# Signs of the last seven weight pieces, made on ScalarE and multiplied in by GpSimd

## The chip, the cores and the metric

The kernel runs on one core of a Trainium2 chip. The metric is the device time of one execution in microseconds (us). Engines are named as in the profile: PE (TensorE), with PEld for its weight loads, DVE (VectorE), ACT (ScalarE), POOL (GpSimd) and SP (SyncE, which issues transfers).

## What is computed

Three stages follow each other. The first is a gated linear attention over 768 positions of 4 batches with 8 heads of width 40; the second sends each of 3072 tokens to one of eight experts with a capacity of 384; the third is a dense layer with ELU between two weight matrices.

```python
for t in range(S):
    m_new = np.maximum(f_gate[:, :, t] + m, i_gate[:, :, t])
    f_stab = np.exp(f_gate[:, :, t] + m - m_new)
    i_stab = np.exp(i_gate[:, :, t] - m_new)
    C = f_stab[..., None, None] * C + i_stab[..., None, None] * np.einsum('bhd,bhe->bhde', vt, kt)
    n = f_stab[:, :, None] * n + i_stab[:, :, None] * kt
    y[:, :, t] = sigmoid(o_gate[:, :, t]) * einsum(C, qt) / np.maximum(np.abs(nq), 1.0)
...
out[mask] = np.maximum(x[mask] @ w1[e], 0.0) @ w2[e]
...
h = x @ w_in
g = np.where(h > 0.0, h, np.exp(np.minimum(h, 0.0)) - 1.0)
return g @ w_out
```

The two dense matrices `w_in` and `w_out` arrive as 64-bit floats. The kernel needs each as a sum of two 32-bit parts (high and low), so it has to turn 64-bit words into 32-bit ones first.

## The kernel before

**Attention** runs 24 steps (`Attention.run`, u = 0 to 23), each on 64 positions of two batches. In program order, which is also each engine's order, a step u issues: PE the recall of the next step and the scores of the one after it (L415, L311), a zeroing matmul (L385); DVE the weighting P (L380) and the seed of the output (L391) for the next step; PE the logits (L484), then the values and the state update (L401, L428); DVE the gates (L448 to L453) and the state sum C (L439); POOL the scaled output x (L454); PE a transpose of the former x (L470) and the decay (L322, L327), which ACT turns into xT (L472) and W (L329); POOL kt (L368), C (L370), and in every second step the mask product sel (L341). In every fourth step ACT also makes `keep` (L488) for a transpose of PE that comes ahead of the decay.

**Weights beside attention.** `Mlp.win_pieces` is a generator that makes 15 pieces of the dense weights while attention runs. Pieces 0 to 9 are of `w_in` (512 columns), 10 to 14 are of `w_out` (448 columns). `Attention.run` pulls it by `fill()` four times in each step from u = 2 on: once ahead of the gates and three times behind kt and C. Each `yield` ends what one such pull issues, so a pull decides in which place of every engine's order an instruction stands. One piece goes through `conv` (ACT: the absolute value into g, L1010, and a byte of the low word into F, L1017; DVE: the first xor with the sign bits, L1023, and in the next pull the second xor with g, L1026). In the pull after that ACT copies F as the high part (L1086, L1092 and L1094, or L1082), and then the low part is subtracted: by POOL for pieces 0 to 7 (L1088), by DVE for pieces 8 and 9 (L1096, L1098) and 10 to 14 (L1084). `conv` has a second way (`sign=True`), which `wout_pieces` already uses for nine later pieces of 320 columns: ACT also makes the Sign of the high word (L1012), and POOL multiplies it in (L1029).

Steps and pieces meet as follows in the trace: the xors of piece 8 stand behind the gates of step 12 (gates start at 91.86 us); of piece 9 on both sides of step 14's (102.92); piece 10 around those of 16 (114.73), piece 11 around those of 17 (118.78), piece 12 behind 18 (123.79), piece 13 behind 19 (130.14), piece 14 behind 20 (135.15) and ahead of 21's (139.71).

The buffers: `cx` (the 64-bit words) has three, `cg` and `cF` two each. The planner's estimates (`on`) in `conv` shape no order within attention.

Of the kernel before, what the change touches and what calls it, by code (L numbers as in the profile page):

```python
# [36 lines left out]
class Plan:  # L37
# [20 lines left out]
    def on(self, e, ns, after=0):  # L58

        self.at[e] = max(self.at[e], self.t, after) + ns  # L60
        return self.at[e] + HOP
# [899 lines left out]
class Mlp:  # L961
# [38 lines left out]
    def conv(self, wide, tiles, sign=False, top=False):  # L1000


        nc = self.nc
        x, g, F = tiles
        if not wide:
            return
        n = x.shape[1]
        hi = x[:, :, 1]
        on = self.plan.on
        nc.scalar.activation(g, hi.bitcast(F32), AF.Abs, scale=2.0**-112)  # L1010
        if sign:
            nc.scalar.activation(hi.bitcast(F32), hi.bitcast(F32), AF.Sign)  # L1012
        t = on("a", 967 if sign else 474)
        Fi = F.bitcast(I32)
        if top:
            b = x.rearrange("p n t -> p (n t)").bitcast(mybir.dt.uint8).rearrange("p (n t) -> p n t", t=8)
            nc.scalar.activation(Fi, b[:, :, 3], AF.Copy, scale=1 / 32, bias=-31 / 64)  # L1017
        else:
            nc.vector.tensor_scalar(Fi, x[:, :, 0], 29, None, op0=ALU.logical_shift_right)
            on("d", 310)  # L1020
        yield t, "d"
        if not sign:
            nc.vector.scalar_tensor_tensor(Fi, hi, -2**31, Fi, op0=ALU.bitwise_and, op1=ALU.bitwise_xor)  # L1023
            on("d", 484)
            yield self.plan.t, "d"
        nc.vector.scalar_tensor_tensor(Fi, g.bitcast(I32), 3, Fi, op0=ALU.logical_shift_left, op1=ALU.bitwise_xor)  # L1026
        t = on("d", 484)
        if sign:
            nc.gpsimd.tensor_tensor(F, F, hi.bitcast(F32), op=ALU.mult)  # L1029
            t = on("p", 890, t)  # L1030
        yield t, "ad"
# [7 lines left out]
    def win_pieces(self, stage):  # L1039

        nc = self.nc
        A, G = nc.scalar, nc.gpsimd
        wide = self.win.dtype != F32
        n = 512
        al, lo, up = slice(0, 128), slice(0, 64), slice(64, 128)
        tiles = {}
        total = 10 + EARLY * 320 // 448
        self.piece = self.got = 0

        def whole():  # L1050
            return stage.tile([128, n], F32, name="cF")

        def get(i):
            cs = slice(i * n, i * n + n)
            tiles[i] = [stage.tile([128, n, 2], I32, name="cx", bufs=3) if wide else None, None, None if wide else whole()]
            if i >= 10:
                cs = slice((i - 10) * 448, (i - 10) * 448 + 448)
                tiles[i] = [t if t is None else t[:, :448] for t in tiles[i]]
                loads = [(al, self.src(self.wout, al, cs))]
            else:  # L1060
                loads = [(al, self.src(self.win, al, cs))]
            self.fetch(loads, wide, tiles[i])

        def pull():
            if self.got < min(total, self.piece + 2 + wide):
                get(self.got)
                self.got += 1

        self.pull = pull
        for i in range(total):  # L1070
            self.piece = i
            while i not in tiles:
                yield
            k, h = divmod(i, 4)
            cs = slice((i - 10) * 448, (i - 10) * 448 + 448) if i >= 10 else slice(h * n, h * n + n)
            if wide:
                w = 448 if i >= 10 else n
                tiles[i][1:] = stage.tile([128, n], F32, name="cg")[:, :w], whole()[:, :w]
            F = tiles[i][2]
            yield from self.conv(wide, tiles.pop(i), top=True)  # L1080
            if i >= 10:
                A.activation(self.first[0][:, cs], F, AF.Copy)  # L1082
                yield
                nc.vector.tensor_tensor(self.first[1][:, cs], F, self.first[0][:, cs], op=ALU.subtract)  # L1084
            elif k < 2:
                A.activation(self.wih[:, k, cs], F, AF.Copy)  # L1086
                yield
                G.tensor_tensor(self.wil[:, k, cs], F, self.wih[:, k, cs], op=ALU.subtract)  # L1088
            else:
                w = self.wis.rearrange("p (k e t) -> p k e t", e=2, t=128)[:, 4 * h:4 * h + 4]  # L1090
                F = F.rearrange("p (k t) -> p k t", t=128)
                A.activation(w[lo, :, 0], F[lo], AF.Copy)  # L1092
                yield
                A.activation(w[up, :, 1], F[up], AF.Copy)  # L1094
                yield
                nc.vector.tensor_tensor(w[up, :, 0], F[lo], w[lo, :, 0], op=ALU.subtract)  # L1096
                yield
                nc.vector.tensor_tensor(w[lo, :, 1], F[up], w[up, :, 1], op=ALU.subtract)  # L1098
            yield
# [641 lines left out]
```

## Time and profile before

| What | Value |
|---|---|
| three runs | 745.18, 745.80, 748.81 us, median 745.80 |
| profiled execution | 748.99 us, of it 747.2 us span |
| attention | to about 152 us of the span |
| busy in the span | PE 697.8, DVE 558.0, ACT 395.5, POOL 198.9 us |
| busy from 0 to 152 us | PE 127.35, DVE 125.27, ACT 76.50, POOL 87.43 us |
| granted clock, mean | 0.970 |

The averages over the span hide the stages: behind attention PE is busy almost without a pause, and inside it several engines take turns. Each row of a timeline tells the start, the reported duration, the engine, the line, and what is written from what; in brackets stands how long the engine was idle ahead of it and which instruction ended that. Reported durations of neighbours can overlap by some hundredths.

### The profile page before, as it was taken

The numbers are of one execution on the slowest core, as the hardware profiler recorded it, in microseconds if no ns is written. First come the engines' busy times: TensorE is split into PE (matmuls) and PEld (weight loads), VectorE is DVE, ScalarE is ACT, GpSimd is POOL, SyncE is SP. The second block draws the span as 40 slices with busy tenths as digits, with TensorE's granted clock in tenths as the row PEclk, the third lists the DMA queues.
The fourth block names the chain that finished last, engine by engine and source line by source line (L and its number), as shares of the span: only waits on it lengthen the run. The fifth ranks groups of instructions, "written<-read, shape, count | busy, mean of one in ns | idle before, by whom it ended". The sixth has DMA issues, their size and how long they took to land.

```text
span 747.2 us, 17816 instructions
## 1 busy us (share of the span) xinstructions
PE 697.8 (93%) x7106; PEld 638.2 (85%) x7118; DVE 558.0 (75%) x1656; ACT 395.5 (53%) x894; POOL 198.9 (27%) x251
## 2 busy tenths in 40 slices
PE   7779889846999999999999999999999999999997
PEld 4656566635989998999899999999999999999997
DVE  8686999876888978986897688778867863752542
ACT  5544555434454727662675367456736763752443
POOL 5665766336211400410121022104100441001001
PEclk9998999955999999999999999999999999999999
DMA  8776878236101400410230023003200532100000
GB/s 280 237 211 195 262 237 257 65 115 195 41 1 52 157 1 1 139 62 10 73 109 28 1 86 97 28 1 114 72 25 1 172 106 76 37 1 27 1 1 26
DMA packets 21634, 67.28 MB, mean 90 GB/s; under 512 B 3504, under 2 KB 6576, under 8 KB 21552
## 3 DMA queue, kind: packets, MB, share of 16 engines
q1 hardware_dynamic: 13440, 35.12, 15.3%
q0 software_dynamic: 8064, 30.94, 12.6%
q8 instruction: 55, 0.90, 0.5%
q14 instruction: 27, 0.22, 0.1%
q10 hardware_dynamic: 48, 0.10, 0.0%
HBM read 58.28 MB, written 7.86 MB: 89 GB/s over the span
## 4 chain that ended last, share of the span: by engine, by line
PE 64%; issue 9%; DVE 7%; ACT 2%; DMA 2%; POOL 2%; POOLq 0%; SPq 0%; ACTq 0%; DVEq 0%
PE ph L1270 30%; PE acc L1423 6%; PE acc L1415 6%; PE acc L1416 6%; PE acc L1371 2%; PE acc L1365 2%; PE acc L1366 2%; PE acc L1363 1%; PE acc L1372 1%; DMA xd<-x 1%; PE ph L1223 1%; PE pr L843 1%; DMA stg<-in_w1b_dram,wi 1%; DVE e L1323 1%; POOL out_dram L1452 1%
## 5 line engine op out<-in xcount | busy, mean ns | idle before, releaser
L1323 DVE SCALAR_TENSOR_TENSOR e<-e,ph 128x384 f32<-128x384 f32 x128 | 70.1, 549 | 46.1 <-ACT e L1320 45.6
L1319 ACT ACTIVATE e<-ph 128x384 f32<-128x384 f32 x128 | 62.4, 487 | 76.5 <-PE ph L1270 66.6
L1270 PE MATMUL ph<-yh,wih 128*128 128x384 f32 x256 | 87.7, 343 | 0.0
L1270 PE MATMUL ph<-yh,wil 128*128 128x384 f32 x256 | 86.3, 337 | 0.0
L1147 DVE TENSOR_TENSOR gl<-e,gh 128x384 fp32r<-128x384 f32 x128 | 69.9, 550 | 2.3 <-ACT gh L1140 1.0
L1287 ACT ACTIVATE gh<-ph 128x384 fp32r<-128x384 f32 x62 | 30.5, 492 | 74.3 <-PE ph L1270 74.1
L1320 ACT ACTIVATE e<-e 128x384 f32<-128x384 f32 x128 | 67.3, 526 | 4.0
L1452 POOL DMA_INDIRECT out_dram<-ot,idx x24 | 24.7, 1031 | 160.3 <-ACT ot L1140 157.3
L1151 POOL DMA_INDIRECT stg<-in_w1a_dram,wi x16 | 16.0, 997 | 191.4 <-DVE wi L897 188.6
L1270 PE MATMUL ph<-yl,wih 128*128 128x384 f32 x256 | 65.2, 341 | 0.0
L1294 DVE SCALAR_TENSOR_TENSOR gl<-ph,gh 128x384 fp32r<-128x384 f32 x64 | 35.0, 552 | 38.5 <-ACT gh L1287 38.2
L1415 PE MATMUL acc<-woh,gh 128*128 128x320 f32 x186 | 56.2, 313 | 0.0
L1140 ACT ACTIVATE gh<-e 128x384 fp32r<-128x384 f32 x95 | 48.8, 514 | 13.4 <-DVE e L1323 13.2
L1416 PE MATMUL acc<-wol,gh 128*128 128x320 f32 x186 | 55.5, 309 | 0.0
L1415 PE MATMUL acc<-woa,gh 128*128 128x320 f32 x168 | 51.8, 318 | 0.5 <-DVE gh L1142 0.5
L1416 PE MATMUL acc<-wob,gh 128*128 128x320 f32 x168 | 50.4, 309 | 0.0
L1270 PEld LDWEIGHTS ph<-yh,wih 128*128 128x128 f32 x256 | 48.1, 188 | 0.2
L1270 PEld LDWEIGHTS ph<-yh,wil 128*128 128x128 f32 x256 | 48.2, 188 | 0.0
L1270 PEld LDWEIGHTS ph<-yl,wih 128*128 128x128 f32 x256 | 45.5, 188 | 0.0
L1270 PE MATMUL ph<-xh,w1h 128*128 128x384 f32 x128 | 43.6, 341 | 0.9 <-ACT xh L1140 0.7
L1270 PE MATMUL ph<-yh,wis 128*128 128x384 f32 x128 | 44.0, 344 | 0.0
L1270 PE MATMUL ph<-yl,wis 128*128 128x384 f32 x128 | 43.2, 337 | 0.0
(318 smaller groups left out, 2057.8 us busy)
## 6 DMA issues: line engine op xcount, KB each, us to landing
vk<-in_vk_dram SPq DMA_DIRECT2D x24, 484.0 KB, 5.0
qk<-in_qk_dram SPq DMA_DIRECT2D x20, 320.0 KB, 4.2
cx<-in_win_dram SPq DMA_DIRECT2D x10, 512.0 KB, 5.0
xd<-x SPq DMA_DIRECT2D x48, 80.0 KB, 3.5
wx<-in_wout_dram SPq DMA_DIRECT2D x9, 320.0 KB, 2.9
cx<-in_wout_dram SPq DMA_DIRECT2D x5, 448.0 KB, 4.7
qk<-in_qk_dram SPq DMA_DIRECT2D x4, 512.0 KB, 6.6
xg<-xd,idx POOLq DMA_INDIRECT x24, 3.2
```

The lines of the kernel that those rows point to most:

```text
L1140: self.nc.scalar.activation(out, x, AF.Copy)
L1147: self.nc.vector.tensor_tensor(out, x, y, op=ALU.subtract)
L1270: PE.matmul(p, w, x, start=k == 0, stop=k == 7)
L1287: nc.scalar.activation(h, p, AF.Relu)
L1294: nc.vector.scalar_tensor_tensor(l, p, 0.0, h, op0=ALU.max, op1=ALU.subtract)
L1319: nc.scalar.activation(e, p, AF.Relu, scale=-1.0)
L1320: nc.scalar.activation(e, e, AF.Exp, scale=-1.0)
L1323: nc.vector.scalar_tensor_tensor(e, e, -1.0, p, op0=ALU.add, op1=ALU.max)
L1415: PE.matmul(p, h[:, c], wh, start=f == 0, stop=False)
L1416: PE.matmul(p, h[:, c], wl, start=False, stop=False)
L1423: PE.matmul(p, l[:, c], wh, start=False, stop=False)
L1452: s = nc.gpsimd.indirect_dma_start(out=self.out, out_offset=bass.IndirectOffsetOnAxis(ap=idx[:, t:t + 1], axis=0), in_=o, in_offset=None)
```

## The change

`conv` is now called with `sign` true for pieces 8 to 14 of `win_pieces`. Those pieces lose the first xor; ACT makes the Sign of the high word in place; the second xor moves into the pull where the first stood; POOL multiplies F by the signs in the next pull, where the second xor stood. One more `yield` keeps the number of pulls per piece.

```diff
@@ -1026,6 +1026,8 @@
         t = on("d", 484)
         if sign:
+            if top:
+                yield t, "d"
             nc.gpsimd.tensor_tensor(F, F, hi.bitcast(F32), op=ALU.mult)
             t = on("p", 890, t)
         yield t, "ad"
@@ -1077,7 +1079,7 @@
             F = tiles[i][2]
-            yield from self.conv(wide, tiles.pop(i), top=True)
+            yield from self.conv(wide, tiles.pop(i), i >= 8, True)
```

Apart from these instructions no engine's order changes, neither in attention nor behind it. Lines from L1029 on are two higher afterwards.

DVE in step 17, before: the xors of piece 11 (`cF`) stand on either side of the gates (`rd`, `x`) and the state sum, and the low part (`wob`) follows at once.

```order
L1023 SCALAR_TENSOR_TENSOR cF<-cx,cF 128x448
L448 TENSOR_SCALAR rd<-pO 128x8
L449 SCALAR_TENSOR_TENSOR rd<-pO,rd 128x8
L450 RECIPROCAL rd<-rd 128x8
L453 SCALAR_TENSOR_TENSOR x<-sg,pO 128x320
L439 TENSOR_TENSOR C_171<-C_171,pC 128x8x41
L1026 SCALAR_TENSOR_TENSOR cF<-cg,cF 128x448
L1084 TENSOR_TENSOR wob<-cF,woa 128x448
L380 TENSOR_TENSOR P<-pS,W 128x512
```

The same place now:

```order
L1026 SCALAR_TENSOR_TENSOR cF<-cg,cF 128x448
L448 TENSOR_SCALAR rd<-pO 128x8
L449 SCALAR_TENSOR_TENSOR rd<-pO,rd 128x8
L450 RECIPROCAL rd<-rd 128x8
L453 SCALAR_TENSOR_TENSOR x<-sg,pO 128x320
L439 TENSOR_TENSOR C_171<-C_171,pC 128x8x41
L1086 TENSOR_TENSOR wob<-cF,woa 128x448
L380 TENSOR_TENSOR P<-pS,W 128x512
```

The remaining xor stands ahead of the gates, and nothing stands any more between the state sum and the low part.

POOL from step 17 to the x of step 18, before:

```order
L454 TENSOR_TENSOR x<-x,rd 128x320
L368 TENSOR_TENSOR kt_183<-vk,W 128x8x40
L370 TENSOR_TENSOR C_174<-C_173,De 128x8x41
L341 TENSOR_TENSOR sel<-mask,fp 96x512
L454 TENSOR_TENSOR x<-x,rd 128x320
```

And now:

```order
L454 TENSOR_TENSOR x<-x,rd 128x320
L368 TENSOR_TENSOR kt_183<-vk,W 128x8x40
L370 TENSOR_TENSOR C_174<-C_173,De 128x8x41
L341 TENSOR_TENSOR sel<-mask,fp 96x512
L1031 TENSOR_TENSOR cF<-cF,cx 128x448
L454 TENSOR_TENSOR x<-x,rd 128x320
```

The multiply of piece 11 has come in behind sel and ahead of the next x; the ACT copy `woa` that DVE's `wob` reads comes after it.

## Rows read from the trace of the kernel before

**Rows 1.** Window: its us, busy PE PEld DVE ACT POOL, clock, DMA share, GB/s.

```profile
97.21:139.71 42.50, 38.68 (x1098) 27.15 (x1102) 40.76 (x89) 22.53 (x48) 24.52 (x26) 1.00 0.72 215
```

**Rows 2.** Groups on DVE, 92 to 140 us: busy us, mean ns | idle.

```profile
L1026 DVE SCALAR_TENSOR_TENSOR cF<-cg,cF 128x448 int32<-128x448 int32 x5 | 4.5, 896 | 0.0
...
L1026 DVE SCALAR_TENSOR_TENSOR cF<-cg,cF 128x512 int32<-128x512 int32 x2 | 2.2, 1094 | 0.0
```

**Rows 3.** Timeline of POOL and DVE, steps 15 and 16: start, us, instruction.

```profile
112.04 0.75 POOL L370 TENSOR_TENSOR C<-C,De 128x328 f32<-128x328 f32 x1
112.06 1.20 DVE L1023 SCALAR_TENSOR_TENSOR cF<-cx,cF 128x448 int32<-128x448 int32 x1
...
114.19 0.61 DVE L1026 SCALAR_TENSOR_TENSOR cF<-cg,cF 128x448 int32<-128x448 int32 x1
114.73 0.15 DVE L448 TENSOR_SCALAR rd<-pO 128x8 f32<-128x8 f32 x1
```

**Rows 4.** Prices by line (ns min/median/max, first and last start); the table load.

```profile
L1029 POOL TENSOR_TENSOR wt<-wt,wx x8: 867/878/937, 158.7 to 220.7; 128x320 f32<-128x320 f32 x8
L1088 POOL TENSOR_TENSOR wil<-cF,wih x8: 1262/1271/1720, 33.0 to 92.5; 128x512 fp32r<-128x512 f32 x8
L1012 ACT ACTIVATE wx<-wx x8: 483/496/502, 153.6 to 217.8; 128x320 f32<-128x320 f32 x8
L150 ACT ACT_TABLE_LOAD x1 | 1.3, 1283 | 1.2 <-PEq L1731 1.2
```

**Rows 5.** Timeline of steps 12 to 14: POOL, ACT, PE, DVE.

```profile
92.49 1.27 POOL L1088 TENSOR_TENSOR wil<-cF,wih 128x512 fp32r<-128x512 f32 x1
...
95.48 0.63 ACT L1092 ACTIVATE wis<-cF 64x512 fp32r<-64x512 f32 x1 [1.68 <-DVE cF L1026]
...
98.19 0.60 ACT L329 ACTIVATE W<-pF 128x512 f32<-128x512 f32 x1 [0.42 <-PE pF L327]
...
101.81 0.55 PE L470 MATMUL pX<-ident,x 128*128 128x128 f32 x3
...
102.92 0.15 DVE L448 TENSOR_SCALAR rd<-pO 128x8 f32<-128x8 f32 x1
```

**Rows 6.** Timeline around step 17: three POOL instructions, then undisturbed ones, ACT, DVE.

```profile
119.88 0.72 POOL L454 TENSOR_TENSOR x<-x,rd 128x320 f32<-128x320 f32 x1 [1.56 <-DMA xd<-x]
120.56 1.12 POOL L368 TENSOR_TENSOR kt<-vk,W 128x320 f32<-128x320 f32 x1
121.64 0.75 POOL L370 TENSOR_TENSOR C<-C,De 128x328 f32<-128x328 f32 x1
...
101.30 1.15 POOL L341 TENSOR_TENSOR sel<-mask,fp 96x512 bf16<-96x512 bf16 x1
131.92 0.74 POOL L368 TENSOR_TENSOR kt<-vk,W 128x320 f32<-128x320 f32 x1
...
121.11 0.58 ACT L1082 ACTIVATE woa<-cF 128x448 fp32r<-128x448 f32 x1 [0.32 <-DVE cF L1026]
122.79 0.68 DVE L380 TENSOR_TENSOR P<-pS,W 128x512 f32<-128x512 f32 x1
123.79 0.15 DVE L448 TENSOR_SCALAR rd<-pO 128x8 f32<-128x8 f32 x1
```

**Rows 7.** Timeline of steps 14, 18 and 19 to 21: POOL, DVE, ACT.

```profile
104.01 0.72 POOL L454 TENSOR_TENSOR x<-x,rd 128x320 f32<-128x320 f32 x1 [1.56 <-ACT W L329]
...
108.39 0.68 DVE L1096 TENSOR_TENSOR wis<-cF,wis 64x512 fp32r<-64x512 f32 x1
...
124.88 0.72 POOL L454 TENSOR_TENSOR x<-x,rd 128x320 f32<-128x320 f32 x1 [0.99 <-DMA xd<-x]
...
129.61 0.62 DVE L1084 TENSOR_TENSOR wob<-cF,woa 128x448 fp32r<-128x448 f32 x1
...
134.26 0.58 ACT L1082 ACTIVATE woa<-cF 128x448 fp32r<-128x448 f32 x1 [2.60 <-DVE cF L1026]
...
137.62 0.62 DVE L1023 SCALAR_TENSOR_TENSOR cF<-cx,cF 128x448 int32<-128x448 int32 x1 [0.18 <-ACT cF L1017]
```

## Prediction

> **What bounds the kernel now.** All edited instructions lie in attention, whose last steps end at about 152 us, so I read that stage first. The busy times over the stretch that holds eight steps and most of the edits [rows 1] show DVE at 40.76 of 42.50 us and PE at 38.68, with POOL and ACT at little more than half. DVE is therefore the engine to relieve, and PE stands close behind it: 42.50 less 38.68 leaves 3.8 us at most before PE is the bound. Next I read single instructions. The second xor (L1026) takes 896 ns at 448 columns and 1094 ns at 512 [rows 2], yet an undisturbed one holds DVE for 0.54 us only, from 114.19 to the next start at 114.73 [rows 3]. The reader should see why in the same group: the first xor at 112.06 overlaps a POOL instruction that ends at 112.79 and then runs for just its own half microsecond, to 113.26. So an instruction of DVE with two operands in SBUF waits for the POOL instruction in flight, and the reverse holds too: kt on POOL takes 0.74 us alone and 1.12 beside an xor [rows 6]. Last I read the chains around three waits: steps 12 to 14 [rows 5], step 17 [rows 6], and steps 14, 18 and 19 to 21 [rows 7].
>
> The Trainium skill, page "SBUF — State Buffer", section "Who interferes with whom", speaks against this change: DVE with two SBUF inputs and a GpSimd instruction that reads SBUF exclude each other for a whole instruction, whichever began first. The trace agrees (the xor of 112.06 above took 1.20 us). By that rule the multiply put on POOL is paid for a second time wherever DVE meets it; without it the seven freed slots would be pure gain.
>
> **What is removed.** Per piece one of two xors goes. The remaining one moves up into the place of the first, where it meets the same POOL instruction; what really disappears is the old slot of L1026. Two of 1094 and five of 896 ns make 6.7 us [rows 2]; reported durations run 0.07 us past the next start (0.61 against 0.54, rows 3), so DVE loses 6.2 us.
>
> **What is added.** Seven Signs on ACT: 496 ns at 320 columns [rows 4], a copy at 448 is 0.58 [rows 6], so about 0.55 each, 3.8 us on an engine that is half idle. No table change comes with them: the run loads one table [rows 4], and Sign already runs eight times later on. (The Trainium skill, page "ScalarE: Activation LUTs", section "Table sets: the hidden batching unit", does not name sign among the functions that every set holds; two loads of its 2.66 us for each Sign would be an estimate of 37 us. The single load in the trace excludes it.) Seven multiplies on POOL: the same operation takes 878 ns at 320 columns, a 512-wide subtract 1271 ns [rows 4]. Scaled by columns that is between 1.11 and 1.23 us at 448 and between 1.27 and 1.40 at 512; I take 1.2 and 1.35, nearer the multiply, which reads the same strided sign. POOL has the time; the question is where the multiply stands.
>
> **Where it stands.** On POOL each multiply is behind x, kt, C (and every second step sel) of a step and ahead of the next x. On ACT the copy of its result (L1092, L1082) stands ahead of the next W, xT and conversions, and on DVE the low part (L1096, L1084) follows. Until now the copy waited for DVE; now it waits for POOL's queue. I follow the start of the gates (L448) step by step and note how late it is against before.
>
> Step 12 to 14 (piece 8): POOL is free of L1088 at 93.76 [rows 5]; then come the remaining xor 0.57, x 0.72, kt 0.74, C 0.75 and the multiply 1.35, less small overlaps: 97.7. The ACT copy that started at 95.48 starts 2.2 us later. From that copy to W (98.19) ACT took 2.7 us, five short instructions and two waits on PE, of which I estimate 2.0 as work; so W comes at 99.7 and PE's next recall, in order behind that step's decay, starts 1.7 us later. PE had finished the values of step 14 at 101.8, the gates waited for DVE until 102.92: 1.04 us of cover. The gates of step 14 are **0.65 late**, although a DVE slot has gone.
>
> Step 15 (piece 9): x starts at 104.01 [rows 7], now 104.66; x 0.72, kt 0.74, C 0.75, one DVE instruction that takes the operand path between them 0.57, multiply 1.35, copy 0.63 end at 109.4, less overlaps 109.1. The low part on DVE, ahead of the gates, started at 108.39. The slot freed in step 14 is eaten: **0.7 late**.
>
> Steps 16 and 17 (piece 10): the slot before the gates of step 16 was an undisturbed 0.54, so 0.2 late; then the copy waits for the multiply and one more Sign stands before the conversion that step 17's xor needs: **0.5 late**.
>
> Step 17 to 18 (piece 11) is the largest term. After the change DVE's order is gates, C, low part (L1084), P. The low part needs, all behind these gates on POOL, x 0.72, kt 0.74, C 0.75, sel 1.15, the multiply 1.2, then the ACT copy 0.58, and takes 0.55 itself: 5.7 us from the start of x at 119.88, so P starts at 125.6, where it stood at 122.79 [rows 6]. DVE has nothing else to do in this time; everything behind it, P, the seed and the gates of step 18 (123.79), is 2.8 us later: **3.3 late** in all.
>
> Step 18 to 19 (piece 12): x, kt, C, the xor 0.54, small DVE instructions 0.2, multiply 1.2 and copy 0.58 after x at 124.88 plus 3.3 end at 132.9; the low part before the gates started at 129.61 [rows 7]. The 1.1 us of the freed slot is eaten again: **3.4 late**. Steps 19 to 22 (pieces 13, 14): a slot of 1.0 gives 0.6 back in step 20 (the conversion, late on ACT, takes 0.4). But the copy of piece 13, at 134.26 [rows 7], now follows x, kt, C, the xor, sel and a multiply, to about 139.8, and behind it xT, W and three conversions (0.5 us apart) delay the xor that stands in the place of 137.62 by some 5 us; with one xor less behind it, the gates of step 21 are 4.5 late. The last steps have no state to update, DVE has less to do there than PE, and I let them give 0.7 back (an estimate): **3.8 late** at the end of attention. Routing and the expert stages follow in series and are unchanged.
>
> **The sum.** Waits of 10.0 us against 6.2 us freed: plus 3.8. The profiled execution took 748.99 (span 747.2), 3.2 above the median of 745.8; I add to the median: 749.6. The multiply's two prices move five of these chains by 0.1 each, and each hand-over is good to some 0.3, so this case alone spans 747.5 to 752.
>
> **Rivals.** *The two cancel* (746.8). PE and ACT hide their waits: the late W of step 13 and the late conversion of step 20 cost nothing, taking 1.65 and 1.1 off. For it: ACT is idle half of the time. Against it: PE runs almost without a pause in these steps. It decides at whether PE's recall of step 14 starts before 99.5. *Faster* (742.0). The mechanism is DVE's relief: if the copy of each piece is ready when its low part is reached, all 6.2 us leave DVE and PE's 3.8 us of room [rows 1] is the gain. For it speaks the busy share of DVE, against it the order of step 17. The point is whether multiply 11 ends before the C update of that step. *Slower still* (752). The multiply starts just ahead of DVE's larger two-operand instructions, so they wait 1.2 us in steps 14 and 18 where I let DVE go first, 2.4 us more. That the change does not do what it says I exclude: one xor fewer and one multiply more per piece stand in the built order.
>
> **How the numbers follow.** Forecast 0.46, cancel 0.28, slower still 0.15, faster 0.11. About 0.5% (3.7 us) is what a measurement of this kernel can tell from no change, and my forecast lies on that bound: a little over half of its case and all of the slower one make 0.42 for slower; most of the faster case makes 0.09; 0.49 remains. The range runs from 743.5 (part of the faster case left out) to 753.5 (the slower case with its hand-overs).
>
> **What would show it.** The line L1023 loses seven at 128x512 and 128x448, POOL gains seven multiplies near 1.2 to 1.4 us. The step right or wrong: in step 17 a DVE idle of about 3 us before L1084, released by the ACT copy, itself idle for the multiply; the copy of piece 8 idle for POOL, W of step 13 near 99.7; the gates of steps 14, 18 and 22 late by 0.65, 3.3 and 3.6. If the gates of step 18 are no later than 124.5, or the copy waits fall together with idle PE, the forecast is wrong, and the cancelling or the faster case holds.

## The result, and the profile after

| | median | fastest to slowest | ratio to before [95%] |
|---|---|---|---|
| before | 745.89 us | 744.50 to 749.27 (7 runs) | |
| after | 750.72 us | 749.41 to 753.01 (7 runs) | 1.0059 [1.0040, 1.0079] |

The change costs 4.83 us of the median; 749.6 was forecast.

The two profiled executions hide this at first: 748.99 us before, 749.41 after. The difference lies ahead of the first edited instruction, where the code is the same. The gates of step 12 started at 91.86 us before and at 86.91 after; over all profiled executions told of here that time ranges from 86.4 to 91.9. Part of this goes with the clock: ahead of step 12 the mean granted clock was 0.94 in before, 0.98 in after, and 1.00 in the two executions with the earliest gates (86.44 and 86.64). So I compare the stretch from the gates of step 12 to those of step 23, which holds all seven pieces. Where nothing in them differs, its steps repeat from execution to execution to some 0.02 us in most cases; pauses of PE (up to 0.5 us in a step) and a fall of the clock (1.08) make the exceptions told below. The stretch took **55.02 us before and 59.74 after: plus 4.72**, and that agrees with the 4.83 of the medians, whose interval is 3.0 to 5.9 us.

Windows over that stretch, of before and then of after (columns as in [rows 1]):

```profile
91.86:146.88 55.02, 50.19 (x1357) 36.10 (x1361) 50.35 (x114) 28.49 (x61) 30.88 (x33) 1.00 0.65 192
```

```profile
86.91:146.65 59.74, 51.95 (x1363) 36.22 (x1361) 44.51 (x107) 31.50 (x68) 36.54 (x40) 0.97 0.58 178
```

DVE is busy 5.8 us less, ACT 3.0 and POOL 5.7 more: the work has moved as planned. But DVE's idle time went from 4.7 to 15.2 us, and 10.6 us more idle less 5.8 less work is the 4.72. Groups by line in that stretch of after (busy us, mean ns of one | idle ahead of them and what ended most of it):

```profile
L1031 POOL TENSOR_TENSOR cF<-cF,cx 128x448 f32<-128x448 f32 x5 | 5.7, 1149 | 3.2 <-issue 3.2
L1031 POOL TENSOR_TENSOR cF<-cF,cx 128x512 f32<-128x512 f32 x2 | 2.6, 1278 | 0.0
...
L1026 DVE SCALAR_TENSOR_TENSOR cF<-cg,cF 128x448 int32<-128x448 int32 x5 | 4.6, 925 | 1.9 <-ACT cF L1017 1.9
L1086 DVE TENSOR_TENSOR wob<-cF,woa 128x448 fp32r<-128x448 f32 x5 | 4.2, 846 | 6.5 <-ACT woa L1084 6.5
...
L1012 ACT ACTIVATE cx<-cx 128x448 f32<-128x448 f32 x5 | 3.1, 615 | 0.2
L1084 ACT ACTIVATE woa<-cF 128x448 fp32r<-128x448 f32 x5 | 2.9, 575 | 11.3 <-POOL cF L1031 11.3
L1012 ACT ACTIVATE cx<-cx 128x512 f32<-128x512 f32 x2 | 1.3, 670 | 0.1
L1094 ACT ACTIVATE wis<-cF 64x512 fp32r<-64x512 f32 x2 | 1.3, 630 | 7.1 <-POOL cF L1031 7.1
```

The low part of pieces 10 to 14 and the copies in the stretch of before, for comparison (their lines are two lower there):

```profile
L1084 DVE TENSOR_TENSOR wob<-cF,woa 128x448 fp32r<-128x448 f32 x5 | 4.3, 860 | 1.7 <-ACT woa L1082 1.7
L1082 ACT ACTIVATE woa<-cF 128x448 fp32r<-128x448 f32 x5 | 2.9, 576 | 5.5 <-DVE cF L1026 5.5
L1092 ACT ACTIVATE wis<-cF 64x512 fp32r<-64x512 f32 x2 | 1.3, 630 | 3.3 <-DVE cF L1026 3.3
```

The idle times are to be read as a chain. DVE's low part (L1086) waited 6.5 us for ACT's copy (L1084), where it had waited 1.7; that copy waited 11.3 us, and piece 8's and 9's copies (L1094) 7.1, for the multiply on POOL (L1031), where they had waited 5.5 and 3.3 for the xor on DVE. In [rows 2] the xor of L1026 had no idle time ahead of it; the one that is left waits 2.5 us for a byte conversion that ACT reaches later (L1017).

| step from gates to gates | 12 | 13 | 14 | 15 | 16 | 17 | 18 | 19 | 20 | 21 | 22 |
|---|---|---|---|---|---|---|---|---|---|---|---|
| before, us | 5.35 | 5.71 | 6.19 | 5.62 | 4.05 | 5.01 | 6.35 | 5.01 | 4.56 | 4.04 | 3.13 |
| after less before | -0.47 | +1.17 | +0.33 | -0.54 | +0.47 | **+2.60** | +0.49 | -1.10 | **+2.04** | -0.63 | +0.36 |

Step 17, in the timeline of after: POOL, then ACT, then DVE. It answers to [rows 6].

```profile
115.87 0.72 POOL L454 TENSOR_TENSOR x<-x,rd 128x320 f32<-128x320 f32 x1 [1.94 <-DMA xd<-x]
116.56 0.73 POOL L368 TENSOR_TENSOR kt<-vk,W 128x320 f32<-128x320 f32 x1
117.25 0.75 POOL L370 TENSOR_TENSOR C<-C,De 128x328 f32<-128x328 f32 x1
117.95 1.15 POOL L341 TENSOR_TENSOR sel<-mask,fp 96x512 bf16<-96x512 bf16 x1
119.06 1.15 POOL L1031 TENSOR_TENSOR cF<-cF,cx 128x448 f32<-128x448 f32 x1
...
120.25 0.58 ACT L1084 ACTIVATE woa<-cF 128x448 fp32r<-128x448 f32 x1 [3.93 <-POOL cF L1031]
...
115.66 0.49 DVE L439 TENSOR_TENSOR C<-C,pC 128x328 f32<-128x328 f32 x1
120.86 0.62 DVE L1086 TENSOR_TENSOR wob<-cF,woa 128x448 fp32r<-128x448 f32 x1 [4.70 <-ACT woa L1084]
121.40 0.68 DVE L380 TENSOR_TENSOR P<-pS,W 128x512 f32<-128x512 f32 x1
```

POOL runs x, kt, C, sel and the multiply without a gap. Nothing in that row is slow; the multiply is only fifth in it. DVE, with nothing else in front of the low part, stands still for 4.70 us.

### The profile page after: what moved, and what is told of

It is laid out like the page before. It is cut to its first block, busy times and chain, and to the rows that moved or that the text cites. A ratio compares the mean times of both kernels' runs of the same rounds, so it can differ in the third digit from the quotient of the medians.

```text
span 747.6 us, 17814 instructions
## 1 busy us (share of the span) xinstructions
PE 697.0 (93%) x7118; PEld 637.5 (85%) x7118; DVE 556.3 (74%) x1649; ACT 398.2 (53%) x901; POOL 204.2 (27%) x258
## 4 chain that ended last, share of the span: by engine, by line
PE 64%; issue 8%; DVE 5%; ACT 2%; POOL 1%; DMA 1%; POOLq 0%; ACTq 0%
PE ph L1272 30%; PE acc L1425 6%; PE acc L1417 6%; PE acc L1418 6%; PE acc L1373 2%; PE acc L1367 2%; PE acc L1368 2%; PE acc L1365 1%; PE acc L1374 1%; PE ph L1225 1%; PE pr L843 1%; DVE e L1325 1%; DMA stg<-in_w1b_dram,wi 1%; POOL out_dram L1454 1%; PE pX L482 1%
## 5 line engine op out<-in xcount | busy, mean ns | idle before, releaser
L1418 PE MATMUL acc<-wol,gh 128*128 128x320 f32 x186 | 55.5, 309 | 0.0
```

The costliest lines, as they stand in the source:

```text
L1418: PE.matmul(p, h[:, c], wl, start=False, stop=False)
```

## The experiments

Each was made on the changed kernel, but e4_sign_only and e5_mult_only on the kernel before. The stretch is that from the gates of step 12 to those of step 23, in the one profiled execution of each; the ratio is that of the whole runs to runs of before measured along with them, whose medians lay between 746.3 and 747.3 us. The whole runs scatter by more than most of these effects, since the part ahead of step 12 varies by up to 5 us; the verdicts therefore rest on the steps. A sum over the stretch is less sure than its steps: e9_not11_13 and e12_not11_13_again are the same kernel, and their sums differ by 1.20 us. And in three runs the interval of the whole runs does not hold the difference of the stretch: it is -2.3 to +0.7 us in e3_mult_early (stretch +2.82), -1.0 to +1.5 in e1_not11 (+1.77) and -3.4 to -1.0 in e7_no_waiting (-0.71). What else differed there, outside the stretch or from execution to execution, is not shown.

| run | stretch, us | less before | median, us | ratio [95%] |
|---|---|---|---|---|
| e1_not11 | 56.79 | +1.77 | 746.88 | 1.0003 [0.9987, 1.0020] |
| e2_only11 | 58.13 | +3.11 | 748.59 | 1.0025 [1.0005, 1.0046] |
| e4_sign_only | 55.06 | +0.04 | 747.57 | 1.0004 [0.9983, 1.0024] |
| e5_mult_only | 57.24 | +2.22 | 747.83 | 1.0010 [0.9984, 1.0036] |
| e6_one_xor | 54.57 | -0.45 | 744.24 | 0.9975 [0.9950, 1.0000] |
| e7_no_waiting | 54.31 | -0.71 | 745.04 | 0.9971 [0.9955, 0.9987] |
| e3_mult_early | 57.84 | +2.82 | 746.86 | 0.9989 [0.9969, 1.0009] |
| e8_copy_later | 57.94 | +2.92 | 747.99 | 1.0022 [0.9996, 1.0048] |
| e10_only8 | 56.22 | +1.20 | 747.15 | 0.9996 [0.9967, 1.0024] |
| e11_only8_later | 55.24 | +0.22 | 746.07 | 1.0005 [0.9987, 1.0022] |
| e9_not11_13 | 57.61 | +2.59 | 747.15 | 1.0011 [0.9987, 1.0035] |
| e12_not11_13_again | 56.41 | +1.39 | 747.14 | 1.0012 [0.9993, 1.0031] |

### Is step 17's wait piece 11's own?

The theory: the multiply of piece 11 stands fifth on POOL, and DVE has nothing ahead of the low part. The rival: the step is late because earlier pieces have made it so, or because POOL as a whole has too much. Piece 11 alone goes back to two xors, and then piece 11 alone is changed.

```diff
-            yield from self.conv(wide, tiles.pop(i), i >= 8, True)
+            yield from self.conv(wide, tiles.pop(i), i >= 8 and i != 11, True)   # e1_not11
+            yield from self.conv(wide, tiles.pop(i), i == 11, True)              # e2_only11
```

> As the changed kernel, but piece 11 keeps both its xors on DVE; six pieces have the multiply. Theory (the cost is the place of a multiply in POOL's queue, and piece 11 pays most of it, since DVE reaches its low part straight after the gates): DVE's idle of 4.70 us ahead of the low part of step 17 goes; from the gates of step 12 to those of step 23 it takes 57.1 us (before 55.02, changed 59.74), total about 748. Rival (each multiply costs alike, through POOL's load and the operand path that DVE shares with it): six sevenths of 4.7 us stay, 59.0 us in the stretch, total about 750.

> Only piece 11 gets the Sign and the multiply; the other six keep both xors. Theory: this piece alone brings about 2.6 us, 57.6 us from the gates of step 12 to those of step 23, total 748.5. Rival (each multiply costs alike): 0.7 us, 55.7 us, total 746.6, which the runs would hardly tell from before.

Step 17 grew by -0.01 us in e1_not11 and by +2.62 in e2_only11, against +2.60 in after. The low part in that step, in e1_not11 and then in e2_only11:

```profile
117.28 1.14 DVE L1086 TENSOR_TENSOR wob<-cF,woa 128x448 fp32r<-128x448 f32 x1 [0.64 <-ACT woa L1084]
```

```profile
121.61 0.63 DVE L1086 TENSOR_TENSOR wob<-cF,woa 128x448 fp32r<-128x448 f32 x1 [4.71 <-ACT woa L1084]
```

The wait comes with piece 11 and goes with it, whatever the other six do. The theory stands, and this one piece makes well over half of the loss. The 0.5 us by which e2_only11 lies above its expectation goes with a pause of PE in step 15, taken up in the last section.

### What do Signs, multiplies, relief and waits cost by themselves?

Four kernels take the change apart. Unread results go to a scratch tile that was made from three tiles of the set-up. e4_sign_only: both xors stay, ACT makes seven unread Signs. e5_mult_only: both xors stay, POOL makes seven unread multiplies in the place of the new ones. e6_one_xor: the first xor goes, and no Sign or multiply comes. e7_no_waiting: everything is issued as in the change, but the multiply writes elsewhere and nobody reads it.

```diff
-        if sign:
+        if sign and not top:                                                     # e6: no Sign
             nc.scalar.activation(hi.bitcast(F32), hi.bitcast(F32), AF.Sign)
...
+        if junk is not None:                                                     # e4: 7 Signs more
+            nc.scalar.activation(junk, hi.bitcast(F32), AF.Sign)
...
+        if junk is not None:                                                     # e5: 7 multiplies more
+            nc.gpsimd.tensor_tensor(junk, g, hi.bitcast(F32), op=ALU.mult)
...
-            nc.gpsimd.tensor_tensor(F, F, hi.bitcast(F32), op=ALU.mult)
+            if not top:                                                          # e6
+                nc.gpsimd.tensor_tensor(F, F, hi.bitcast(F32), op=ALU.mult)
+            nc.gpsimd.tensor_tensor(self.router.cj[:, :n] if top else F, F,      # e7
+                                    hi.bitcast(F32), op=ALU.mult)
```

> The kernel before with both xors and, for pieces 8 to 14, a Sign on ACT that writes a tile which nothing reads, in the place that the change gives it. Theory: ACT has idle time in front of the instructions behind it, 0 to 0.5 us from the gates of step 12 to those of step 23 (55.0 to 55.5). Rival (ACT's longer queue costs by itself): 0.5 us per piece, 58 us and more.

> The kernel before with both xors, and for pieces 8 to 14 a multiply on POOL in the place that the change gives it; it reads g and the high word and writes a tile that nothing reads, so no engine waits for its result, and no Sign is made. Theory: POOL had room, so only the meetings with DVE's two-operand instructions and a later x cost, 0.3 to 1.3 us from the gates of step 12 to those of step 23 (55.3 to 56.3), total about 746.7. Rival (the shared operand path and POOL's load are the cause): 3 us and more, over 58 us in the stretch.

> Pieces 8 to 14 lose the first xor as in the changed kernel, but get neither Sign nor multiply: the signs of these weights are left out. This is what the relief of DVE is worth alone. Theory: DVE gets 6.2 us back, and PE, which stood 3.8 us under the length of eight steps, becomes the bound: 51.0 to 52.0 us from the gates of step 12 to those of step 23 (before 55.02). Rival (DVE was never what held these steps): 54.5 to 55.

> All that the change puts on ACT and POOL is issued in its places, and DVE has one xor less, but the multiply writes a tile that nothing reads, and the copies of pieces 8 to 14 read what the xor left: the signs are left out of these weights and nothing waits for the multiply. Theory: relief (to 51 or 52) plus the 2.2 us that the multiplies alone cost in the run above, so about 54 us from the gates of step 12 to those of step 23; the remaining 5.7 us of the changed kernel's 59.74 are waits for the result. Rival (the work itself, on the shared operand path, is the loss): 57 us and more.

**e4_sign_only**: 55.06, as expected. Signs are free here.

**e5_mult_only**: 57.24, between theory and rival. Nearly all of it stands in steps 14 (+1.15) and 18 (+1.03). In step 14 the multiply and DVE's comparison ask for their operands together; POOL and DVE of that moment:

```profile
102.41 1.28 POOL L1030 TENSOR_TENSOR cj<-cg,cx 128x512 f32<-128x512 f32 x1
...
102.42 1.83 DVE L728 TENSOR_TENSOR g<-b,thr 128x512 bf16<-128x512 f32 x1
```

The comparison, 0.68 us long where nothing meets it, waits out the multiply. So work on POOL that nobody reads is not free where DVE meets it.

**e6_one_xor**: 54.57, the rival's value. Relief of DVE without any added work or wait was worth **0.45 us** in this stretch, not 3 or 4 (in the whole runs 0.0 to 3.7). DVE was busy 44.83 us of it, 5.5 less than before, but idle 5.1 more. Steps 12 to 15 together gained 1.54, steps 16 and 17 lost 1.68 again. The gates of steps 17 and 18 in its DVE timeline:

```profile
114.50 0.17 DVE L448 TENSOR_SCALAR rd<-pO 128x8 f32<-128x8 f32 x1 [0.52 <-PE pC L428]
...
120.19 0.17 DVE L448 TENSOR_SCALAR rd<-pO 128x8 f32<-128x8 f32 x1 [1.60 <-PE pC L428]
```

Here DVE waits for PE. And PE, in the midst of the matmuls that the gates wait for, stood still itself:

```profile
113.88 0.27 PE L401 MATMUL pO<-vk,P 64*64 64x64 f32 x2 [0.65 <-issue]
...
119.35 0.27 PE L401 MATMUL pO<-vk,P 64*64 64x64 f32 x2 [0.81 <-issue]
```

"Issue" means that the profile shows nothing that PE waited for. What goes with these pauses is told in the last section. Since they stand in this run and not in before, the 0.45 is no upper bound of what relief can give.

**e7_no_waiting**: 54.31, as expected: 0.71 less than before with all the added work in it. Against after, where the same instructions are waited for, that is 5.43 us less. So of the change **5.43 us hang on waiting for the multiply's result, and everything else together is a gain of 0.71.** The whole runs of the two kernels bear out the first number: their ratios, 1.0059 and 0.9971, lie 0.88% apart, which is some 6.6 us. The second number holds a loss of its own: in step 18, which grew by 1.32, the xor met three POOL instructions in a row. DVE, then POOL:

```profile
118.70 2.61 DVE L1027 SCALAR_TENSOR_TENSOR cF<-cg,cF 128x448 int32<-128x448 int32 x1
...
118.71 0.72 POOL L454 TENSOR_TENSOR x<-x,rd 128x320 f32<-128x320 f32 x1
119.39 0.73 POOL L368 TENSOR_TENSOR kt<-vk,W 128x320 f32<-128x320 f32 x1
120.08 0.75 POOL L370 TENSOR_TENSOR C<-C,De 128x328 f32<-128x328 f32 x1
```

Ahead of x on POOL stands the multiply of piece 11 (117.60 to 118.75), so that x, kt and C run without a gap. In after the same xor took 1.01 us. The 5.43 is therefore the net of two kernels that also meet on the operand path in different places.

### Does it help to move the multiply, or the copy?

e3_mult_early issues the multiply in the pull of the xor, for all pieces; on POOL that moves the multiplies of pieces 9 and 11 alone: that of 9 from behind kt and C of step 14 to ahead of that step's x, that of 11 from behind sel of step 17 to ahead of that step's x. e8_copy_later puts a pull between multiply and copy, for all seven.

```diff
-            if top:
-                yield t, "d"
             nc.gpsimd.tensor_tensor(F, F, hi.bitcast(F32), op=ALU.mult)
             t = on("p", 890, t)
+            if top:                              # e3_mult_early
+                yield t, "d"
...
+        if sign and top:                         # e8_copy_later
+            yield t, "ad"
```

> All seven pieces as in the changed kernel, but the multiply is issued in the same pull as its xor, one pull earlier; the number of pulls stays. Only for pieces 9 and 11 does that change POOL's order: their multiply stands ahead of x of steps 14 and 17 where it stood behind sel and C. The work on every engine is that of the changed kernel. Theory: the idle of DVE in step 17 falls from 4.70 us to under 1, steps 12 to 23 take about 56.5 us (the other waits on ACT remain), total about 747.5. Rival (the amount of work on POOL and ACT costs, not its place): 59.7 us and 750.7 stay.

> The changed kernel with one more pull between the multiply and ACT's copy for pieces 8 to 14, so that the copy, and the low part behind it, stand a quarter of a step later in every queue, and each later piece starts one pull later. Nothing is left out. Theory: most of the waits for the multiply go and DVE's relief is left, less the 2.2 us of meetings: 53.5 to 55.5 us from the gates of step 12 to those of step 23, total between 744.5 and 746.5, so equal to before or a little faster. Rival (the waits only move with the copy): 58 us and more, total about 750.

**e3_mult_early**: 57.84, 1.90 better than after, 1.3 short of what I expected. The wait of the low part in step 17 fell from 4.70 to 1.01 us; but then the gates of step 18 waited for PE:

```profile
120.34 0.62 DVE L1086 TENSOR_TENSOR wob<-cF,woa 128x448 fp32r<-128x448 f32 x1 [1.01 <-ACT woa L1084]
...
123.93 0.17 DVE L448 TENSOR_SCALAR rd<-pO 128x8 f32<-128x8 f32 x1 [1.95 <-PE pC L428]
```

with a pause in PE's values just ahead of it, of the same kind as in e6_one_xor:

```profile
123.10 0.27 PE L401 MATMUL pO<-vk,P 64*64 64x64 f32 x2 [1.09 <-issue]
```

**e8_copy_later**: 57.94 against 53.5 to 55.5 expected, so the rival's 58. My theory falls here, in so far as it took the waits to end where the copy comes late enough. They went with the copy to other places; three of them in its DVE timeline:

```profile
117.59 0.17 DVE L448 TENSOR_SCALAR rd<-pO 128x8 f32<-128x8 f32 x1 [1.88 <-PE pC L428]
...
121.16 1.64 DVE L1026 SCALAR_TENSOR_TENSOR cF<-cg,cF 128x448 int32<-128x448 int32 x1 [1.26 <-ACT cF L1017]
...
138.24 0.63 DVE L1026 SCALAR_TENSOR_TENSOR cF<-cg,cF 128x448 int32<-128x448 int32 x1 [1.88 <-ACT cF L1017]
```

Ahead of the first, PE paused for 0.38 us (at 116.98) as in e6_one_xor. 1.28 us of the sum stand in step 22, in whose second half a granted clock of 0.50 shows (window 146.0 to 147.0 us); without them it would be 56.7, still far above the expectation.

### Piece 8, alone and with a later copy

```diff
-            yield from self.conv(wide, tiles.pop(i), i >= 8, True)
+            yield from self.conv(wide, tiles.pop(i), i == 8, True)               # both
...
-                A.activation(w[lo, :, 0], F[lo], AF.Copy)                        # e11: for piece 8
                 yield
+                A.activation(w[lo, :, 0], F[lo], AF.Copy)                        # one pull later
                 A.activation(w[up, :, 1], F[up], AF.Copy)
```

> Only piece 8 gets Sign and multiply, issued as in the changed kernel. Theory (its copy blocks ACT ahead of keep and W): gates of step 13 come 0.46 earlier and of step 14 0.70 later than before, counted from those of step 12, and with DVE full behind them that stays: 55.7 us to the gates of step 23. Rival (the loss in step 13 came from the next piece's Sign): 54.6.

> Only piece 8 gets Sign and multiply, and both its copies on ACT are issued together one pull later, behind keep and the tanh of step 13; no other instruction moves. Nothing is left out. Theory: the freed slot of DVE is kept, gates of step 14 come 0.4 to 0.5 earlier than before, counted from those of step 12, 54.5 to 54.7 us to the gates of step 23 (before 55.02, with the copies in their old place 55.7); in the total that is under what the runs can tell, about 747. Rival (the copies hold up W as much from the later place): 55.3 and more.

e10_only8: step 12 shortened by 0.46, step 13 lengthened by 1.18; the gates of step 14 come 0.72 late, as worked out. Nearly all of the rest of its 1.20 is one step, 16, with 0.45 and a pause of PE in it. e11_only8_later: step 13 lengthened by 0.68 instead of 1.18. The later copy saves some two fifths of the loss of step 13, and the piece still gains nothing: +0.22, next to the rival's value and not the theory's. In its ACT timeline the first copy waits for the multiply even so, 1.43 us, and W stands behind both copies:

```profile
94.16 0.63 ACT L1098 ACTIVATE wis<-cF 64x512 fp32r<-64x512 f32 x1 [1.43 <-POOL cF L1031]
...
95.56 0.59 ACT L329 ACTIVATE W<-pF 128x512 f32<-128x512 f32 x1
```

That is 7.12 us after the gates of step 12 (88.44), against 6.33 before and 7.60 in after.

### Piece 13 and step 20

```diff
-            yield from self.conv(wide, tiles.pop(i), i >= 8, True)
+            yield from self.conv(wide, tiles.pop(i), i in (8, 9, 10, 12, 14), True)
```

> As the changed kernel, but pieces 11 and 13 keep both xors on DVE; pieces 8, 9, 10, 12 and 14 have Sign and multiply. It tests the reading of step 20, where the changed kernel lost 2.04 us: ACT's copy of piece 13 waited for its multiply and held up the conversion of piece 14. Theory: step 20 loses 0.5 us or less against before, step 19 no longer gains its 1.1, and from the gates of step 12 to those of step 23 it takes 56.0 to 56.4 us (56.79 with only piece 11 left out). Rival (piece 14's own Sign and multiply hold up step 20): step 20 still loses 1.5 us or more, 57.3 us and above.

> The same kernel as e9_not11_13, pieces 11 and 13 as before the change, once more. In e9_not11_13 step 13 grew by 2.25 us, in the changed kernel and with piece 11 alone undone by 1.17 or 1.18. The rows of e9_not11_13 show a granted clock of 0.50 from 95.11 to 98.11 us, which lies in that step, and 1.00 in the same place of the changed kernel. If the extra 1.08 us are the clock's, an execution in which the granted clock stays at 1.00 through the stretch has step 13 at +1.17 and the stretch from gates 12 to gates 23 at 56.5 us. If they belong to the kernel (the order of its instructions), step 13 is +2.25 again at a clock of 1.00 and the stretch is 57.6 us. Step 20 stays within 0.1 us of before by either.

Step 20 grew by 0.03 us in the first and by 0.03 in the second, against +2.04 in after and in e1_not11. The chain is the predicted one: piece 13's copy behind the multiply, and behind that copy the conversion for piece 14. In step 20 of after, ACT and DVE:

```profile
135.09 0.58 ACT L1084 ACTIVATE woa<-cF 128x448 fp32r<-128x448 f32 x1 [3.87 <-POOL cF L1031]
...
138.21 0.62 DVE L1026 SCALAR_TENSOR_TENSOR cF<-cg,cF 128x448 int32<-128x448 int32 x1 [1.88 <-ACT cF L1017]
```

But against e1_not11 the stretch is only 0.38 us shorter (56.41 and 56.79), since step 19 no longer gives its 1.1 back and step 21 not its 0.6.

In e9_not11_13 step 13 grew by 2.25 us, where after, e1_not11, e3_mult_early and e10_only8 show 1.17 or 1.18. A window of it shows what was different, and the same window of the second execution of the same kernel (7.0 to 10.0 us after the gates of step 12) bears it out:

```profile
95.11:98.11 3.00, 2.78 (x49) 1.87 (x51) 1.64 (x3) 2.33 (x5) 0.95 (x2) 0.50 1.00 365
```

```profile
94.60:97.60 3.00, 2.73 (x73) 1.74 (x73) 1.84 (x4) 2.74 (x6) 1.66 (x3) 1.00 0.91 329
```

The granted clock was 0.50 in the first and 1.00 in the second; PE got through 49 matmuls instead of 73 in the same 3 us, and in the second step 13 took 6.89 us (+1.18). So the extra 1.08 us goes with the clock, not with the kernel.

## Why the prediction was right, step by step

How late the gates were, against those of step 12, beside what was worked out:

| gates of step | 14 | 15 | 16 | 17 | 18 | 19 | 20 | 21 | end |
|---|---|---|---|---|---|---|---|---|---|
| predicted | 0.65 | 0.7 | 0.2 | 0.5 | 3.3 | 3.4 | 2.8 | 4.5 | 3.8 |
| measured | 0.70 | 1.03 | 0.49 | 0.96 | 3.56 | 4.05 | 2.95 | 4.99 | 4.72 |

**Steps 12 to 14 held in each link.** W of step 13 was to come 1.5 us later than [rows 5] show it, measured from the gates of step 12 (99.7 against 98.19). It came 1.27 later: 94.51 less 86.91 is 7.60, where 98.19 less 91.86 was 6.33. PE's recall was to start 1.7 later; 95.18 less 86.91 is 8.27, where before 98.42 less 91.86 was 6.56, so 1.71. The rows, ACT and PE of after:

```profile
92.61 0.63 ACT L1094 ACTIVATE wis<-cF 64x512 fp32r<-64x512 f32 x1 [3.71 <-POOL cF L1031]
...
94.51 0.59 ACT L329 ACTIVATE W<-pF 128x512 f32<-128x512 f32 x1
...
95.18 0.27 PE L415 MATMUL pR<-C,qk 64*64 64x64 f32 x2
```

The case in which the waits cancel the gain was tied to a recall before 99.5 us. In the time of before's trace 95.18 is 100.13, so by its own mark that case was out; e10_only8 shows the same with piece 8 alone.

**Step 17 held in its sum and not in its idle time.** From x to P the prediction counted 5.7 us; the rows above show 5.53 (115.87 to 121.40). The step grew by 2.60, where 2.8 was worked out. DVE's idle time was to be about 3 us and was 4.70: before, the second xor and a slow low part stood in that gap, and work that leaves a gap makes the wait in it longer by as much. The forecast of the delay had this right; the number named for the idle time had not.

**Steps 19 to 21 held in their chain**: 2.04 us in step 20, where the prediction had 1.7 (2.8 to 4.5), and e9_not11_13 ties it to piece 13. Single links are off by 0.3 to 0.5 us in steps 14, 18, 19 and 20 and at the end (where 0.27 came back instead of 0.7; the gates of step 22, forecast 3.6 late, were 4.36 late); all but that of step 19 go the same way, and that is the missing 0.9 us.

**Step 18 went half the way of the slower rival.** The prediction let DVE go ahead of the multiply in steps 14 and 18. In step 14 it did; the comparison met C on POOL and was served first. In step 18 it was not. After, steps 14 and 18, DVE and POOL:

```profile
101.23 0.68 DVE L727 TENSOR_TENSOR g<-b,thr 128x512 bf16<-128x512 f32 x1
...
101.22 1.30 POOL L370 TENSOR_TENSOR C<-C,De 128x328 f32<-128x328 f32 x1
...
125.97 1.15 POOL L1031 TENSOR_TENSOR cF<-cF,cx 128x448 f32<-128x448 f32 x1
...
125.97 1.69 DVE L727 TENSOR_TENSOR g<-b,thr 128x512 bf16<-128x512 f32 x1
```

The comparison paid 1.01 us there. The step grew by 0.49 in all, in after as in e1_not11 (+0.48), so about half of it was covered, as a freed slot of 0.54 would. The Trainium skill, page "SBUF — State Buffer", section "Who interferes with whom", says that the two engines share an exclusive lock and that the order of issue decides who blocks. The rows agree with the lock: the same comparison took 0.68 us when it went first and 1.69 behind a multiply of 1.15. On the order they decide nothing: in both steps the two rows start within some 0.01 us of each other, POOL's ahead, and DVE went first in one and POOL in the other.

**The ledger, "waits of 10.0 us against 6.2 us freed", was wrong in both terms and right in its difference.** The runs give 5.43 us of waits (e7_no_waiting against after) and 0.45 of relief (e6_one_xor), 0.71 with the added work beside it. The mis-sized step is the counting of a freed slot as freed time: in e6_one_xor 5.5 us less work on DVE came with 5.1 us more idle time, 2.1 of it ahead of the gates of steps 17 and 18, and part of that goes with PE's pauses. I had written the growth of waits into the waits and the slots into the gain, and both came out some 5 us too large. They cancel by construction: 10.0 is the 3.8 us of lateness, followed from gate to gate, plus the 6.2. The step-by-step account above, which carries only the lateness of the gates, does not have this error.

**The faster rival found little to gain.** It took PE's 3.8 us of room [rows 1] as the gain that DVE's relief would set free. With no wait for the multiply, e7_no_waiting is 0.71 us shorter, and with no multiply either, e6_one_xor is 0.45 shorter. Its own mark also fell: multiply 11 ended at 120.2, the C update of that step began at 115.66.

**Prices.** The multiply took 1149 ns at 448 and 1278 at 512 columns, in the lower parts of the intervals, where I took 1.2 and 1.35: beside the subtract's 1271 ns at 512 [rows 4] the strided sign operand costs nothing that shows. The Signs took 615 and 670 ns (seven on ACT), a little over my 0.55 us; e4_sign_only shows that they are hidden, and no second table load came:

```profile
L150 ACT ACT_TABLE_LOAD x1 | 1.3, 1283 | 1.2 <-PEq L1733 1.2
```

## What to carry to other kernels

An operation that moves from the busiest engine to an idle one is priced by its place in the new engine's order, and by who reads its result next: here a multiply of 1.15 us, fifth in POOL's row, cost a 2.6 us step. Before a change is built to relieve an engine, run the kernel once with that work simply left out: here it would have shown a gain of 0.45 us in the stretch, from an engine that was busy 92% of it, where 3 to 4 were expected. And where a loop repeats, compare steps from gate to gate, since whole runs hide differences of 1 to 3 us that the steps show to some 0.02; but look for pauses and for the clock in a step before its difference is put down to the edit.

## What the runs showed of the hardware

**PE pauses that follow instruction packets.** In eight of the fourteen profiled executions (seven kernels) PE stops for up to 1.4 us in the middle of the values and state matmuls (L401, L428), with nothing shown that it waits for. Each of the 14 such pauses that I looked up ended 2.23 to 2.63 us after a packet on the DMA queue that the profile names "instruction". Such packets come some 5 us apart, so that a hit in a window of 0.4 us would be chance in one of twelve. Two queue rows of e6_one_xor, from the windows 111.40 to 111.50 and 117.00 to 117.10 us; the pauses that end at 113.88 and 119.35 belong to them:

```profile
q8 instruction: 1, 0.02, 59.3%
```

```profile
q8 instruction: 1, 0.02, 54.9%
```

In before, after, e1_not11, e4_sign_only, e5_mult_only and e7_no_waiting those matmuls have no such pause. Pauses without a shown cause stand ahead of other matmuls too, where they moved no gates that I could see: 0.44 us ahead of L415 in e7_no_waiting (2.42 us after a packet) and 1.83 ahead of L320 in e6_one_xor (2.35 after). One of 0.57 us ahead of L320 in e11_only8_later does not fit: it ended 3.33 us after the last packet. My reading is that PE waits there for its own instructions, and that this takes a part of DVE's relief away in steps 16 and 17 of e6_one_xor (in e7_no_waiting, without such pauses there, these steps together lost 1.74 us less), holds the gates of step 18 in e3_mult_early, and makes the 0.45 to 0.50 us of step 16 in e10_only8 and e2_only11. It rests on the coincidence in time; no run changed the length of PE's program, so the cause stays open. The Trainium skill, page "Runtime: NRT & Kernel Launch", section "Instruction fetch mechanics", says that each engine's program streams in by blocks of 16 KiB (256 instructions) and that the cost of a block's boundary is mostly hidden. The packets of 0.02 MB agree with the size. That it is hidden agrees with before and after; if the reading is right, it does not hold in the eight executions with pauses.

**A DVE instruction can lose the operand path to several POOL instructions in a row.** I had reckoned with one meeting per instruction, as in [rows 3]. The xor of e7_no_waiting above waited out x, kt and C, 2.61 us where an undisturbed one holds DVE for 0.54; POOL had no gap between the three. That alone does not decide it: in e10_only8 a low part on DVE that started at 114.00 us, during x on POOL (113.65, 0.72 us), took 0.85 us, and kt, next on POOL without a gap at 114.33, took 1.12 instead of 0.73, so there DVE went in ahead of the second. Which of the two goes first in a row of several is not shown.

**The granted clock fell in one execution and not in another, after the same pause.** In step 13 PE stands for 1.62 us ahead of a transpose; the row of e9_not11_13 and that of e12_not11_13_again:

```profile
94.66 0.46 PE L492 MATMUL pX<-ident,keep 128*128 128x128 f32 x1 [1.62 <-ACT keep L488]
```

```profile
94.15 0.33 PE L492 MATMUL pX<-ident,keep 128*128 128x128 f32 x1 [1.62 <-ACT keep L488]
```

In the first the clock then was 0.50 (1.2 GHz, the lower of its two levels) for some three microseconds, in the second it stayed at 1.00; what decides is not shown by these runs. In the stretch of after it fell once, following the long wait of step 17 (PE 2.40 us idle, first row), from 123.91 to 126.41 us (second row):

```profile
122.55 0.28 PE L415 MATMUL pR<-C,qk 64*64 64x64 f32 x2 [2.40 <-DVE pO L391]
```

```profile
123.91:126.41 2.50, 2.50 (x25) 1.23 (x27) 2.43 (x5) 0.00 (x0) 2.50 (x4) 0.50 0.78 238
```

There it cost nothing that can be seen: step 18 grew by 0.49 us with it and by 0.48 without it in e1_not11, as DVE had work for 6.70 of that step's 6.84 us. In step 13 of e9_not11_13, where the gates waited for PE, it cost 1.08.
